# The last layers' first weight pieces asked for on GpSimd, and two of them converted ahead of the first square

## The chip, the core and the metric

The kernel runs on one core of a Trainium2 chip. The metric is the device time of one execution in microseconds (us); the median of three runs is taken. A core has TensorE (PE: matrix products; PEld: its weight loads), VectorE (DVE), ScalarE (ACT), GpSimd (POOL) and SyncE (SP), each working through its own queue of instructions in order, and 16 DMA engines that move data between the large memory and the core's own. SP, ACT and POOL can ask for transfers.

## The reference

Three stages, one after the other: an attention over pooled keys and values, a mixture of experts with one expert a token and a limit on the tokens of an expert, and a dense pair of layers. The change lies in the dense pair:

```
def _moe2_ref(x, w_in, w_out, s, b):        # x: 2304 x 512
    h = x @ w_in                            # w_in: 512 x 2048
    r = np.maximum(h, 0.0)
    g = s * (r * r) + b
    return (g @ w_out).astype(np.float32)   # w_out: 2048 x 512
```

The inputs are 64-bit floats in memory. Tokens over an expert's limit have x = 0; their output row is b times the column sums of w_out.

## The kernel before

**Stages.** Attention, then `Experts.main` (the experts' units of 288 tokens, then small units of up to 144), then `last_layers`. Which units exist depends on the routing, so they stand in nested conditionals; `last` closes the small units. It stores the last small unit's result from the tile `yo` (`store_small`, `store_y`, the SP transfer at L1101), and TensorE computes the first four blocks (`EARLY`) of token unit 0 there.

**Precision.** Every product of the dense pair is three matmuls in a 32-bit format: high half times high half, high times low, low times high. Tokens are split into halves by `split_y` (ScalarE casts, L1014; another engine subtracts, L1015). The pieces of `w_out` are split by `split_out`: ScalarE casts (L1374), VectorE subtracts (L1375).

**Converting w_out.** A piece is 128 rows of `w_out`, 512 KB of 64-bit floats, loaded as pairs of integers by `load_out` (L1446). `Weights64.step` makes 32-bit floats of it in four steps: L859, L862 with ScalarE's L861, L864, L868, of which the second also runs `split_out` for the piece before and the third adds the piece before to the column sums (`add`, L1380; for the first piece a copy on ScalarE, L1382). Two integer buffers c_f and one buffer c_u are shared by all pieces. `cvs` holds two such sequences: 14 pieces (59 steps, `steps_of_first`) and 2 pieces. `conv(n, end)` runs the next n steps, up to `end`.

**last_layers.** The 2,048 columns of the first layer are 16 blocks; the second layer sums over the same 16. Token units are 256 wide. `pair` treats units 0 and 1 together, so that the conversion has more to lie beside: `first(u, f0, f1, banks)` computes blocks of the first layer, each followed by `square` (ScalarE's Relu, L1399, and VectorE's product, L1400, which for every third block writes back into the bank) and by one step `conv(1)`; during unit 0 it also splits unit 1's tokens on VectorE (blocks 10 to 13). `parts` of the block before casts it (L1414) and subtracts (L1415, on GpSimd, or on VectorE for every third). `second` is the second layer (`layer2`, L1420) over two token halves, with `conv(2)` after each block. The order is: 16 blocks of unit 0, 7 of unit 1 (`HEAD`), the second layer over 7 blocks for unit 0 and for unit 1, the last two pieces' loads, unit 1's other 9 blocks, and the rest of the second layer. Unit 0's blocks go around all 8 banks, unit 1's around 4. After `pair`, the units from 2 on go one by one.

**Memory.** `last_layers` takes its tiles from a pool `n`, opened where the experts' pools `m` and `m1` stood before they were closed (L1590 to L1598). `m1` held `yo`; `m` held the experts' weights and raw pieces of `w_in`. `onesf`, y1h, y1l, c_f, c_u, gh, gl and the tiles `wo` are in `n`. The order on each queue is the order in which the program is written; waits are put in by the framework.

**Around the change.** In `pair` SP asks for pieces 0 to 5, then the tokens of unit 1 (`load_y(1)`, L1009 and L1010), the scalars s and b (L1455), and pieces 6 to 13. `nc.gpsimd.memset(onesf, 1.0)` (L1459) is GpSimd's first instruction of the stage.

Of the kernel before, what the change touches and what calls it, by code (L numbers as in the profile page):

```python
# [24 lines left out]
P = 128  # L25
# [10 lines left out]
KF2 = FF2 // P  # L36
# [1313 lines left out]
def last_layers(nc, tc, c, a, pool, x, ps, out):  # L1350
# [6 lines left out]
    sb = pool.tile([P, 2], F32, name="sb")  # L1357
# [6 lines left out]
    wo = [pool.tile([P, DM, 2], I32, name=f"wo{i}") for i in reversed(range(KF2))][::-1]  # L1364
# [5 lines left out]
    wout = a["moe2_w_out"].bitcast(I32).rearrange("(k p) c -> p k c", p=P)  # L1370
# [18 lines left out]
    def conv(n, end=len(steps)):  # L1389
        for _ in range(n):  # L1390
            if done[0] < end:
                z, i = steps[done[0]]
                z.step(i)
                done[0] += 1

    def square(f, p, n, inside=False):

        r = rt[f % 4][:, :n]
        nc.scalar.activation(r, p, AF.Relu)  # L1399
        nc.vector.scalar_tensor_tensor(out=p if inside else r, in0=p, scalar=0.0, in1=r, op0=ALU.max, op1=ALU.mult)  # L1400
# [9 lines left out]
    def parts(f, n=CU, u=0, p=None):  # L1410

        h, l = place(f, u)
        r = rt[f % 4][:, :n] if p is None else p
        nc.scalar.copy(h[:, :n], r)  # L1414
        (nc.gpsimd if p is None else nc.vector).tensor_sub(l[:, :n], r, h[:, :n])  # L1415

    def layer2(p, j, f, c=slice(0, DM), u=0):
        h, l = place(f, u)
        for i, (g, z) in enumerate(((h, 0), (h, 1), (l, 0))):
            nc.tensor.matmul(p[:, c], lhsT=g[:, j * P:j * P + P], rhs=wo[f][:, z, c], start=f == 0 and i == 0, stop=f == KF2 - 1 and i == 2)  # L1420
# [12 lines left out]
    def tokens(u):  # L1433
        if u < NV:
            for k in range(KD):
                x.split_y(u, k, nc.gpsimd)
# [5 lines left out]
        nc.vector.tensor_scalar(out=drop, in0=p, scalar1=sb[:, 1:2], scalar2=None, op0=ALU.mult)  # L1442
        nc.sync.dma_start(out=out.rearrange("(n p) d -> p n d", p=P), in_=drop.unsqueeze(1).to_broadcast([P, T // P, DM]))

    def load_out(i):
        nc.sync.dma_start(out=wo[i].rearrange("p c two -> p (c two)"), in_=wout[:, i])  # L1446

    def pair():

        for i in range(KF2 - 2):  # L1450
            load_out(i)
            if i == 5:
                x.load_y(1)
                for j, n in enumerate(("moe2_s", "moe2_b")):
                    nc.sync.dma_start(out=sb[:, j:j + 1], in_=a[n].unsqueeze(0).to_broadcast([P, 1]))  # L1455
        more.extend(pool.tile([P, 2, 2, CU], F32R, name=f"wo{i}") for i in range(KF2 - 2, KF2))
        spare.extend(x.w.tile([P, 2, CU], F32R, name=f"raw{i}") for i in range(3))
        held = []
        nc.gpsimd.memset(onesf, 1.0)  # L1459

        def first(u, f0, f1, banks):
            for n, f in enumerate(range(f0, f1)):
                p = banks[f % len(banks)][:, :CU]
                if u or f >= EARLY:
                    x.layer1_y(u, p, *win[f])
                inside = f % 3 == 2
                square(f, p, CU, inside)
                conv(1, steps_of_first)
                if u == 0 and 10 <= f < 10 + KD:
                    x.split_y(1, f - 10, nc.vector)  # L1470
                if held:
                    parts(*held.pop())
                held.append((f, CU, u, p if inside else None))
            parts(*held.pop())

        def second(u, f0, f1, end):
            for f in range(f0, f1):
                for j in range(2):
                    layer2(po[2 * u + j], j, f, u=u)
                conv(2, end)  # L1480

        steps_of_first, all_steps = cvs[0].total, len(steps)
        first(0, 0, KF2, ps)
        first(1, 0, HEAD, ph)
        x.load_y(2)
        second(0, 0, HEAD, steps_of_first)
        second(1, 0, HEAD, steps_of_first)
        for i in range(KF2 - 2, KF2):
            wo[i] = pool.tile([P, DM, 2], I32, name=f"wo{i}")
            load_out(i)  # L1490
        first(1, HEAD, KF2, ph)
        conv(all_steps, steps_of_first)
        second(0, HEAD, KF2, all_steps)
        tokens(2)
        second(1, HEAD, KF2, all_steps)
        conv(all_steps)
        raw[0:3] = [x.w.tile([P, DM], F32, name=f"raw{i}") for i in range(3)]
        slots.extend(raw[2:4] + [pool.tile([P, DM], F32, name="c_f1")])
        sums["drop"] = pool.tile([P, DM], F32, name="c_u0")

    def unit(u):
        if u == 2:
            pair()
        if u + 1 < NV:
            x.load_y(u + 1)
        for f in range(KF2):
            p = ph[f % 4][:, :CU]
            x.layer1_y(u, p, *win[f])
            square(f, p, CU)
            if f:  # L1510
                parts(f - 1)
            if u == 2:
                if f == 1:
                    rows(ph[(f + 3) % 4])
                elif f > 11:
                    store((f - 12) // 2, f % 2, po[f - 12])
        parts(KF2 - 1)
        tokens(u + 1)
        if u == 2:
            for f in range(len(slots)):  # L1520
                whole(f)
        for j in range(2):
            p = po[2 * (u % 2) + j]
            for f in range(KF2):
                layer2(p, j, f)
            store(u, j, p)
# [93 lines left out]
```

## Time and profile before

| | us |
|---|---|
| median of three runs | 662.55 (661.93 to 668.51) |
| the profiled execution, its own time | 665.48 |
| its span, first to last instruction | 663.8 |
| TensorE busy | 596.7 |
| VectorE busy | 377.2 |
| ScalarE busy | 254.1 |
| GpSimd busy | 241.9 |

The profile is of one execution. Times in the trace count from the span's start. A busy time of TensorE is modelled, since matmuls are pipelined. A name ahead of "<-" is what is written, names behind it what is read. What ended a wait is inferred from semaphore events: where the engine named had long been done, it was another. `pair` runs from about 340 us, the last small unit's store included, to about 445 us.

### The profile page before, as it was taken

How to read it: one execution, taken by the hardware profiler on the slowest of the kernel's cores; microseconds unless marked ns; L12 is line 12 of the kernel's file. 1: busy time of each engine (PE TensorE's matmuls, PEld its weight loads, DVE VectorE, ACT ScalarE, POOL GpSimd, SP SyncE). 2: the span in 40 equal slices, each digit the busy share in tenths (PEclk: the TensorE clock that was granted, in tenths of full speed). 3: DMA queues.
4: the chain of work that ended last, by engine and by line, in shares of the span. 5: the costliest groups of instructions: out<-in, count | busy, mean ns of one | idle time of the engine just before them, and what ended most of it. 6: DMA issues, size and time to landing. Idle time of an engine off the chain costs nothing. (4 is left out here: it accounts for less than half of the span.)

```text
span 663.8 us, 11041 instructions
## 1 busy us (share of the span) xinstructions
PE 596.7 (90%) x4005; PEld 554.0 (83%) x4005; DVE 377.2 (57%) x889; ACT 254.1 (38%) x620; POOL 241.9 (36%) x277
## 2 busy tenths in 40 slices
PE   5778889689999969997999896999999999999886
PEld 5767778579889969997899776889889899898785
DVE  4699788976979977572719999703412022021150
ACT  1344555435555644434317524404214134043030
POOL 5467232532324503213204401214825336044291
PEclk8798789869999998998999898999999999999998
DMA  8988466645736995756438301017210100100000
GB/s 166 206 166 180 116 171 208 207 149 191 260 131 224 295 284 178 246 172 226 148 91 349 124 1 63 1 32 285 90 39 1 48 17 1 48 17 2 35 1 20
DMA packets 67949, 86.10 MB, mean 130 GB/s; under 512 B 24713, under 2 KB 40073, under 8 KB 67856
## 3 DMA queue, kind: packets, MB, share of 16 engines
q1 hardware_dynamic: 57696, 71.34, 35.5%
q10 hardware_dynamic: 7712, 6.84, 3.5%
q0 software_dynamic: 2448, 6.82, 3.3%
q8 instruction: 42, 0.69, 0.4%
q14 instruction: 51, 0.42, 0.2%
HBM read 68.09 MB, written 17.58 MB: 129 GB/s over the span
## 5 line engine op out<-in xcount | busy, mean ns | idle before, releaser
L1420 PE MATMUL bank<-wo,gh 128*128 128x512 f32 (+1 forms) x412 | 119.2, 374 | 1.2 <-ACT wo L1374 1.0
L1415 POOL TENSOR_TENSOR gl<-rt,gh 128x256 fp32r<-128x256 f32 (+1 forms) x96 | 72.6, 761 | 110.3 <-ACT gh L1414 59.2
L1420 PEld LDWEIGHTS bank<-wo,gh 128*128 128x128 f32 x412 | 74.9, 188 | 15.0 <-ACT wo L1374 1.4
L1420 PE MATMUL bank<-wo,gl 128*128 128x512 f32 (+1 forms) x206 | 76.8, 373 | 0.0
L1096 PE MATMUL bank<-hs,w2h 128*128 128x288 f32 (+1 forms) x308 | 69.1, 313 | 6.1 <-issue 5.7
L1427 DVE SCALAR_TENSOR_TENSOR raw<-bank,sb,c_u 128x512 f32<-128x512 f32 (+1 forms) x14 | 9.9, 710 | 85.5 <-PE bank L1420 85.5
L918 POOL TENSOR_TENSOR w1l<-kraw,w1h 128x512 fp32r<-128x512 f32 x24 | 34.0, 1432 | 64.8 <-ACT w1h L914 64.4
L1096 PEld LDWEIGHTS bank<-hs,w2h 128*128 128x128 f32 x308 | 51.3, 194 | 7.1 <-issue 6.5
L1399 ACT ACTIVATE rt<-tq 128x256 f32<-128x256 f32 (+1 forms) x26 | 9.5, 367 | 113.1 <-PE tq L1022 91.1
L1096 PE MATMUL bank<-hs,w2l 128*128 128x288 f32 (+1 forms) x148 | 45.1, 305 | 0.0
L1420 PEld LDWEIGHTS bank<-wo,gl 128*128 128x128 f32 x206 | 38.8, 188 | 6.8
L1400 DVE SCALAR_TENSOR_TENSOR rt<-bank,rt 128x256 f32<-128x256 f32 (+1 forms) x53 | 21.3, 401 | 38.5 <-ACT rt L1399 38.2
L1414 ACT CAST gh<-rt 128x256 fp32r<-128x256 f32 (+1 forms) x96 | 36.6, 381 | 6.5 <-DVE rt L1400 6.5
L926 POOL DMA_INDIRECT xg<-xd,u_idx x23 | 25.8, 1122 | 35.9 <-DVE lt L283 18.7
L1399 ACT ACTIVATE rt<-bank 128x256 f32<-128x256 f32 (+1 forms) x60 | 22.3, 371 | 35.2 <-PE bank L1022 25.7
L1428 POOL DMA_INDIRECT out_dram<-raw,it x12 | 12.0, 1003 | 62.6 <-DVE raw L1427 62.1
L264 PE MATMUL o<-vx,eT 128*128 128x146 f32 (+1 forms) x144 | 23.5, 309 | 7.8 <-DVE lt L283 7.2
L1400 DVE SCALAR_TENSOR_TENSOR rt<-tq,rt 128x256 f32<-128x256 f32 (+1 forms) x24 | 9.6, 400 | 36.4 <-ACT rt L1399 36.4
L1096 PEld LDWEIGHTS bank<-hs,w2l 128*128 128x128 f32 x148 | 28.7, 194 | 0.0
L264 PEld LDWEIGHTS o<-vx,eT 128*128 128x128 f32 (+1 forms) x144 | 20.2, 194 | 9.1 <-issue 7.1
L922 DVE TENSOR_TENSOR w2l<-vraw,w2h 128x512 fp32r<-128x512 f32 x39 | 26.8, 688 | 1.0 <-ACT w2h L921 0.5
L949 PE MATMUL bank<-xs,w1h 128*128 128x288 f32 (+1 forms) x120 | 26.1, 302 | 1.3 <-DVE hs L952 1.3
(485 smaller groups left out, 1723.7 us busy)
## 6 DMA issues: line engine op xcount, KB each, us to landing
kraw<-in_moe_w_dram SPq DMA_DIRECT2D x14, 1024.0 KB
vraw<-in_moe_w_dram SPq DMA_DIRECT2D x14, 1024.0 KB
wo<-in_moe_w_out_dram SPq DMA_DIRECT2D x16, 512.0 KB
c_raw<-in_moe_w_in_dram ACTq DMA_DIRECT2D x13, 512.0 KB
kraw<-in_k_dram SPq DMA_DIRECT2D x8, 576.0 KB
out_dram<-c_u SPq DMA_DIRECT2D x1, 4608.0 KB
q<-in_q_dram SPq DMA_DIRECT2D x16, 256.0 KB
xd<-xr SPq DMA_DIRECT2D x16, 256.0 KB
```

The source lines that it names most:

```text
L264: nc.tensor.matmul(o[:n, p // 2, p % 2 * 2 * VW:p % 2 * 2 * VW + 2 * VW], lhsT=et[:, p, :n], rhs=two_cols(vx[g][:, 2 * p:2 * p + 2]), star ...
L918: eng.tensor_sub(self.w1l[:, i], self.w1(i), self.w1h[:, i])
L922: eng.tensor_sub(self.w2l[i], self.w2r[:, i], self.w2h[i])
L926: self.nc.gpsimd.indirect_dma_start(out=dst, out_offset=None, in_=self.xd[:have], in_offset=bass.IndirectOffsetOnAxis(ap=idx[:n], axis=0), ...
L949: self.nc.tensor.matmul(p, lhsT=l[:, f, k], rhs=r[k], start=n == 0, stop=n == 3 * KD - 1)
L1096: nc.tensor.matmul(py[d][:, :v.n], lhsT=l[f][:, d * P:d * P + P], rhs=r[f], start=f == 0 and i == 0, stop=f == KF - 1 and i == 2)
L1399: nc.scalar.activation(r, p, AF.Relu)
L1400: nc.vector.scalar_tensor_tensor(out=p if inside else r, in0=p, scalar=0.0, in1=r, op0=ALU.max, op1=ALU.mult)
L1414: nc.scalar.copy(h[:, :n], r)
L1415: (nc.gpsimd if p is None else nc.vector).tensor_sub(l[:, :n], r, h[:, :n])
L1420: nc.tensor.matmul(p[:, c], lhsT=g[:, j * P:j * P + P], rhs=wo[f][:, z, c], start=f == 0 and i == 0, stop=f == KF2 - 1 and i == 2)
L1428: i = nc.gpsimd.indirect_dma_start(out=dst, out_offset=bass.IndirectOffsetOnAxis(ap=ids, axis=0), in_=o[:, c], in_offset=None, bounds_chec ...
```

## The change

`load_out` gets the queue as an argument. In `pair` GpSimd asks for pieces 0 to 5; the token load and the scalars are SP's first requests, and pieces 6 to 13 follow them. Ahead of `first(0, ...)` eight conversion steps are put, so that all later calls of `conv` run eight steps further on.

```diff
-    def load_out(i):
-        nc.sync.dma_start(out=wo[i].rearrange("p c two -> p (c two)"), in_=wout[:, i])
+    def load_out(i, queue=nc.sync):
+        queue.dma_start(out=wo[i].rearrange("p c two -> p (c two)"), in_=wout[:, i])
 
     def pair():
 
-        for i in range(KF2 - 2):
+        for i in range(6):
+            load_out(i, nc.gpsimd)
+        x.load_y(1)
+        for j, n in enumerate(("moe2_s", "moe2_b")):
+            nc.sync.dma_start(out=sb[:, j:j + 1], in_=a[n].unsqueeze(0).to_broadcast([P, 1]))
+        for i in range(6, KF2 - 2):
             load_out(i)
-            if i == 5:
-                x.load_y(1)
-                for j, n in enumerate(("moe2_s", "moe2_b")):
-                    nc.sync.dma_start(out=sb[:, j:j + 1], in_=a[n].unsqueeze(0).to_broadcast([P, 1]))
...
         steps_of_first, all_steps = cvs[0].total, len(steps)
+        conv(8)
         first(0, 0, KF2, ps)
         first(1, 0, HEAD, ph)
```

## Rows read from the trace of the kernel before

**Rows 1.** The page: the chain that ended last, by engine.
```profile
PE 29%; issue 5%; POOL 2%; ACT 1%; DVE 1%; another core or an unknown queue 0%; POOLq 0%; ACTq 0%
```

**Rows 2.** Windows: length, busy PE, PEld, DVE, ACT, POOL, granted clock, DMA share, GB/s.
```profile
365.00:370.00 5.00, 1.98 (x14) 1.58 (x14) 5.00 (x11) 2.46 (x8) 2.36 (x2) 0.99 0.78 311
370.00:375.00 5.00, 5.00 (x31) 5.00 (x31) 4.63 (x11) 3.14 (x8) 2.09 (x3) 0.67 0.40 109
...
410.00:415.00 5.00, 3.70 (x19) 3.41 (x20) 5.00 (x11) 3.38 (x9) 2.30 (x3) 0.59 0.00 0
```

**Rows 3.** Timeline of PE, around the token halves: start, us, engine, instruction, [idle before].
```profile
369.00 0.38 PE L1022 MATMUL tq<-y1l,w1h 128*128 128x256 f32 x1 [2.64 <-DVE y1l L1015]
```

**Rows 4.** Timeline of PE, the first layer's last blocks for unit 1.
```profile
410.05 0.38 PE L1022 MATMUL bank<-y1h,w2h 128*128 128x256 f32 x1 [3.81 <-DVE rt L1400]
...
413.52 0.58 PE L1022 MATMUL tq<-y1h,w2h 128*128 128x256 f32 x1 [1.24 <-DVE gl L1415]
...
421.03 0.63 PE L1420 MATMUL bank<-wo,gh 128*128 128x512 f32 x2
```

**Rows 5.** Who waited for whom from 320 to 350 us: total, times, longest.
```profile
POOL onesf L1459 <- ACT rt L1399: 11.9, 1, 11.9
...
DVE c_f L859 <- DMA wo<-in_moe_w_out_dram: 6.0, 1, 6.0
```

**Rows 6.** Timeline of all engines and of DVE: VectorE's first instructions of the stage.
```profile
342.84 0.43 DVE L1400 SCALAR_TENSOR_TENSOR rt<-tq,rt 128x256 f32<-128x256 f32 x1 [3.56 <-ACT rt L1399]
...
349.25 0.43 DVE L859 TENSOR_SCALAR c_f<-wo 128x512 int32<-128x512 int32 x1 [5.99 <-DMA wo<-in_moe_w_out_dram]
349.60 0.42 DVE L1400 SCALAR_TENSOR_TENSOR rt<-misc,rt 128x256 f32<-128x256 f32 x1
349.93 0.68 DVE L862 SCALAR_TENSOR_TENSOR c_f<-wo,c_f 128x512 int32<-128x512 int32 x1
```

**Rows 7.** Timeline of SP's requests.
```profile
341.25 0.39 SPq L1101 DMA_DIRECT2D yt<-yo  x1
345.01 4.25 SPq L1446 DMA_DIRECT2D wo<-in_moe_w_out_dram  x6
349.31 0.64 SPq L1009 DMA_DIRECT2D yr<-yt  x1
```

**Rows 8.** What SP's queue waited for from 340 to 370 us.
```profile
SPq L1446 <- DMA yt<-yo: 1.8, 1, 1.8
```

**Rows 9.** Timeline of POOL.
```profile
344.78 0.21 POOL L1459 MEMSET onesf<- 128x128 f32 x1 [11.91 <-ACT rt L1399]
```

**Rows 10.** Windows of one microsecond (columns as in the windows above).
```profile
344.00:345.00 1.00, 1.00 (x11) 1.00 (x11) 0.00 (x0) 0.22 (x1) 0.21 (x1) 1.00 0.00 0
...
351.00:352.00 1.00, 1.00 (x11) 1.00 (x10) 1.00 (x2) 0.65 (x3) 1.00 (x2) 1.00 1.04 393
```

**Rows 11.** Lines L926 and L1446: duration ns minimum/median/maximum; landing is L926's.
```profile
L926 POOL DMA_INDIRECT xg<-xd,u_idx x23: 927/980/2152, 111.9 to 311.4; - x23
...
DMA to landing us min/median/max: 4.0/6.7/7.9
...
L1446 SPq DMA_DIRECT2D wo<-in_moe_w_out_dram x16: 327/345/1750, 345.0 to 400.6; - x16
```

**Rows 12.** Timeline of DVE: one piece of the conversion, and the later square.
```profile
398.76 0.42 DVE L859 TENSOR_SCALAR c_f<-wo 128x512 int32<-128x512 int32 x1
...
400.14 0.69 DVE L1375 TENSOR_TENSOR wo<-c_f,wo 128x512 fp32r<-128x512 f32 x1 [0.23 <-ACT wo L1374]
400.75 0.68 DVE L864 SCALAR_TENSOR_TENSOR c_f<-wo,c_f 128x512 int32<-128x512 int32 x1
...
402.56 0.42 DVE L859 TENSOR_SCALAR c_f<-wo 128x512 int32<-128x512 int32 x1
...
409.58 0.42 DVE L1400 SCALAR_TENSOR_TENSOR rt<-bank,rt 128x256 f32<-128x256 f32 x1
```

**Rows 13.** The chain that ended last, in order of time: start, us, what.
```profile
418.48 2.72 PE bank L1022 x24
```

## Prediction

> **What bounds the kernel now.** I read the page first: the chain that ended last is for the greatest part TensorE's, so a change counts only where TensorE stands still or is slowed [rows 1]. The windows of five microseconds around the start of the last layers show where that is: TensorE is busy for 2.0 of the 5 us from 365 and for 3.7 of those from 410, and its granted clock falls (0.67 from 370, 0.59 from 410) [rows 2]. In these windows VectorE is busy for 4.6 to 5.0 of 5 us. So VectorE sets the pace here, and TensorE waits for it twice: 2.64 us for the last low half of unit 1's tokens (L1015, the matmul at 369.00) and 3.81 us for a square (L1400 at 409.58, the matmul at 410.05) [rows 3, 4].
>
> VectorE's busy stretch has a sharp beginning. After its first square at 342.84 it waits 6.0 us for the first piece of w_out, and its first conversion step (L859) starts at 349.25 [rows 5, 6]. This idle stretch is what the change could fill.
>
> Why is the piece late? SP issues the store of the last small unit (L1101) at 341.25 and the first w_out load (L1446) at 345.01, after a wait of 1.8 us that the trace puts down to that store's landing [rows 7, 8]. GpSimd's next instruction is as telling: the memset of `onesf` (L1459), a new tile that needs nobody's data, stands ready from 332.87 and starts at 344.78, after 11.9 us [rows 5, 9]. The view names a Relu (L1399) as its releaser, which a fresh constant does not need; the DMA engines were empty from 344 to 345, so the store's bytes had moved by 344, and the memset starts next [rows 10]. I read it so: `onesf`, `wo` and the buffers c_f and c_u all lie in the pool `n`, opened on the memory that `m` and `m1` gave up, and the first instruction of any engine that touches `n` waits until the last user of that memory is done. That last user is the store out of `yo`, a tile of `m1`.
>
> **The change part by part.**
>
> *The six requests on GpSimd.* In program order they take the memset's place as GpSimd's first instruction on pool `n`. By the reading above they wait where the memset waited, until 344.78, not 332.87: they are not ahead of the store in time, only 0.2 us ahead of SP's request of before. Then each has to be issued. No row shows a plain load from GpSimd; the nearest is its gather L926, median 0.98 us of GpSimd an issue [rows 11], against SP's six issues in 4.25 us, 0.35 the median of one. From the end of an SP issue to the first use took 349.25 - 345.36 = 3.89 us [rows 6, 7]. So the first piece is there at 344.78 + 0.98 + 3.89 = 349.65. In its way comes SP, which no longer has to issue the six pieces first: the token load of unit 1 (512 KB), asked for at 349.31 before, goes out at about 345, and 512 KB at the 393 GB/s of [rows 10] is 1.3 us. If all of that goes ahead of the piece it is there at 350.95. I take the middle, 350.3. Bounds from the gather's own landing times, 4.0 to 7.9 us [rows 11]: 348.8 to 352.7. So VectorE starts 1.05 us later than at 349.25 (from -0.45 to +3.45). The other five requests occupy GpSimd to about 351; it has nothing else to do by then (its first subtraction needs the first square), and the memset's 0.21 us move behind them for nothing.
>
> A rule of the Trainium skill speaks against this part: DMA: Bandwidth & Descriptors, section Issuing engines are not separate DMA queues, says that transfers issued by different engines end on the same 16 DMA engines and interleave, so that a second issuer saves only issue time. The same page's fit for a GpSimd load (2.0 us and the bytes over 436 GB/s) makes 512 KB an estimated 3.2 us, by which the first piece would be there at 348.0 and the total below 2.3 us smaller; no row of before shows such a load.
>
> *The remaining SP loads.* `load_y(1)`, the two scalars and pieces 6 to 13 start some 4 to 6 us earlier. The token load's first use stands behind ten blocks of `first`, the pieces' behind the six before them; neither is waited for where VectorE sets the pace, so nothing is gained.
>
> *conv(8) ahead of the first square.* Two pieces are eight steps. From one L859 to the next (398.76 to 402.56) a piece costs VectorE 3.80 us, in which L1375 takes 0.61 to its successor; L1380, of the same shape, is put at as much [rows 12]. The chain that matters is VectorE's, from its first conversion step to the square at 409.58. It is one queue in order and nearly without gaps (a wait of some 0.23 us in each piece, [rows 12]), so its length is the sum of what stands in it, in whatever order. Before, 51 steps stand in it (16 in the first 16 blocks, 7 in the next 7, 14 and 14 in the two `second` calls). After, all 59 steps of the first 14 pieces do, since they run 8 ahead and their number is bounded. The added eight are L868 of piece 12, the four steps of piece 13 with L1375 and L1380 of its predecessor, and the last L1375 and L1380: 0.60 (at the pace of its neighbours) + 3.80 + 0.61 + 0.61 = 5.6 us. And the first square, which ran in the idle stretch before, now stands in the chain: 0.33 us at the pace of its neighbours [rows 6].
>
> The same eight steps no longer stand behind that square. There TensorE waited 1.24 us for a subtraction (L1415) that was queued among them [rows 4]; I count that back.
>
> Sum at 421.03, where TensorE takes up the second layer again [rows 4]: 1.05 + 5.6 + 0.33 - 1.24 = **+5.7 us**. What lies ahead of that on TensorE is hidden by this chain: it finds no free bank at about 352 (eight blocks computed, the first square not before 355.8), and it stands still for some 4 us there, where it ran on before; the token halves (L1015) come about 8 us later. Both are waits for VectorE in the chain already counted. If VectorE were not the bound, they would be the loss themselves.
>
> The profiled execution took 665.48 us with a span of 663.8; the sum makes it 671.2. The median of the runs shown is 662.55 (661.93 to 668.51), 2.9 below; carried over, the prediction is 662.55 + 5.7 = **668.2 us**.
>
> **The rivals.**
>
> *First: the requests are not held by the store* (not slower). What speaks for it is the code: the first pieces are the last tiles of `n` and lie in what was `m`, on weights and raw pieces that nothing reads after 332. Against it stands the memset. Even then VectorE cannot start at 338, because c_f, which its first step writes, is in the pool too and waits as the memset did: it starts at 345.0, 4.25 us earlier instead of 1.05 later: -4.25 + 5.6 + 0.33 - 1.24 = +0.4, 663.0 us. It decides from a first step at 344.6 on downwards; only then is there a gain, and the store's landing excludes that.
>
> *Second: the piece comes later still.* GpSimd's issue takes longer than a gather's, or the piece shares the way with the token load and with SP's pieces 6 onwards for its whole length. At the gather's longest landing, 7.9 us, the step is at 352.7: 3.45 + 5.6 + 0.33 - 1.24 = +8.1, 670.7 us. The gather's median of 6.7 us speaks for it (351.5, +6.9); but gathers ran beside other large loads.
>
> *Third: the clock.* The five blocks from 410.05 to 421.03 are 60 matmuls. Less the wait of 1.24 they took 9.7 us; at the pace of the last 24 of them, 2.72 us [rows 13], they would take 6.8. The other 2.9 us are the clock, which fell to the lower level of 1.2 GHz for a part of them (0.59 granted from 410 to 415) after the stand of 3.81 us [rows 2, 4]. I expect a stand before the same square again, and so the same loss: TensorE gets the last token half 8 us later, at 377, and took 37 us from there to the stand; so it stops at about 414, and the square comes at 416.6. It is a shorter stand, 2.6 us. If the clock holds, 5.7 - 2.9 = +2.8, 665.4 us.
>
> **How the numbers follow.** Forecast (held by the store, first step from 348.8 to 351.2) 0.60; second rival 0.22; third 0.10; first 0.08. About 1% (6.6 us) is what a measurement of this kernel can tell from no change. The forecast reaches from +4.2 to +6.6 in most of its cases, a fifth beyond; with most of the second rival that makes 0.35 for slower by more. Faster by over 1% would need a first step at about 338, and has 0.04 for what I overlook; 0.61 is left for within 1%. The range goes from just below the first rival, 662.5, to past the second's price, 672.5.
>
> **What would show it.** GpSimd's first w_out request starts at 344.8, not near 333; VectorE's first L859 at 349 to 352 with eight steps ahead of its first L1400, at about 355.8; TensorE stands still at 352 and longer before the token halves; the square of block 7 of unit 1 near 416.6, and no conversion step behind it until L1420 resumes near 426.7. I am wrong if the request starts before 342, if L859 starts before 346, or if VectorE's queue shows gaps of several microseconds between its first step and that square, for then it is not a sum.

## The result, and the profile after

The changed kernel takes 672.58 us (median; 670.07 to 675.94) beside 662.24 us (661.36 to 668.51) for the kernel before in the same runs. The ratio is **1.0135** (95% interval 1.0102 to 1.0168), so the change costs 8.9 us (6.8 to 11.1): 1.0135 times the 662.55 us shown before is 671.5 us. The quotient of the two medians alone is 1.0156, inside that interval. The forecast was 668.2. The profiled execution has a span of 670.9 us, against 663.8.

GpSimd, timeline (start, us, engine, line, instruction, count, [idle before <- releaser]):

```profile
344.60 3.26 POOL L1446 DMA_DIRECT2D wo<-in_moe_w_out_dram  x6 [12.52 <-issue]
347.85 0.22 POOL L1460 MEMSET onesf<- 128x128 f32 x1
```

SP, timeline (same columns):

```profile
340.52 0.39 SPq L1101 DMA_DIRECT2D yt<-yo  x1
343.79 0.37 SPq L1009 DMA_DIRECT2D yr<-yt  x1
...
346.89 4.21 SPq L1446 DMA_DIRECT2D wo<-in_moe_w_out_dram  x6
```

The store of the last small unit (L1101) is asked for 0.73 us earlier in this execution than in the one of before [rows 7], so instants are compared below as distances from that store. GpSimd's first request is 4.08 us behind it; SP's was 3.76 behind it [rows 7]. GpSimd stood idle for 12.5 us ahead of it and gained nothing: the request waits where the memset waited [rows 9]. The six requests take 3.26 us, 0.53 us the median of one. SP asks for the tokens 0.8 us ahead of GpSimd's first request, and for the later pieces 2.3 us behind it.

VectorE, timeline (same columns):

```profile
350.83 0.43 DVE L859 TENSOR_SCALAR c_f<-wo 128x512 int32<-128x512 int32 x1 [11.41 <-DMA wo<-in_moe_w_out_dram]
...
356.70 0.42 DVE L1400 SCALAR_TENSOR_TENSOR rt<-tq,rt 128x256 f32<-128x256 f32 x1
...
412.45 0.69 DVE L868 SCALAR_TENSOR_TENSOR c_f<-c_u,c_f 128x512 f32<-128x512 f32 x1
...
417.69 0.69 DVE L1375 TENSOR_TENSOR wo<-c_f,wo 128x512 fp32r<-128x512 f32 x1 [0.74 <-ACT wo L1374]
418.30 0.68 DVE L1380 TENSOR_TENSOR raw<-raw,c_f 128x512 f32<-128x512 f32 x1
418.90 0.42 DVE L1400 SCALAR_TENSOR_TENSOR rt<-bank,rt 128x256 f32<-128x256 f32 x1
...
430.06 0.42 DVE L859 TENSOR_SCALAR c_f<-wo 128x512 int32<-128x512 int32 x1
```

The first conversion step comes 10.31 us behind the store (8.00 before, [rows 6, 7]), the first square stands behind eight steps, and the square of block 7 of unit 1 comes at 418.90 instead of 409.58 [rows 12]. From 412.45 to 418.90 there are 6.45 us of conversion that no longer stand behind that square; no step follows it until 430.06.

TensorE, timeline (same columns):

```profile
357.17 0.80 PE L1022 MATMUL tq<-yhl,w2h 128*128 128x256 f32 x2 [5.69 <-DVE rt L1400]
...
378.87 0.58 PE L1022 MATMUL tq<-y1l,w1h 128*128 128x256 f32 x1 [2.63 <-DVE y1l L1015]
...
419.37 0.58 PE L1022 MATMUL bank<-y1h,w2h 128*128 128x256 f32 x1 [4.38 <-DVE rt L1400]
```

Windows (length, busy PE, PEld, DVE, ACT, POOL, granted clock, DMA share, GB/s):

```profile
355.00:360.00 5.00, 2.83 (x13) 2.83 (x14) 4.96 (x10) 3.77 (x11) 1.57 (x2) 0.64 1.03 419
360.00:365.00 5.00, 5.00 (x30) 4.78 (x30) 5.00 (x10) 2.94 (x9) 2.38 (x3) 0.68 1.03 411
...
420.00:425.00 5.00, 5.00 (x26) 5.00 (x26) 1.52 (x4) 1.74 (x7) 2.08 (x3) 0.53 0.00 0
```

TensorE now stands three times for VectorE: a new 5.69 us before the first square's bank is free, the token halves, and block 7's square, for 4.38 us instead of 3.81 [rows 3, 4]. After each longer stand the granted clock is low (0.64 and 0.68, then 0.53).

Where the time went, with every link read as a difference of instants in the trace (a first step is the first L859, square 7 the square of block 7 of unit 1, and L1420 the instant at which the second layer is taken up again). For the last two kernels, which have no store there, the start is the end of ScalarE's four copies into `yo`, 0.03 us ahead of the store in the others. In the two kernels that move the store it is the first half's request.

| kernel | start | start to first w_out request | request to first step | first step to square 7 | square 7 to L1420 | sum, less before | time by the ratio |
|---|---|---|---|---|---|---|---|
| before | 341.25 | 3.76 | 4.24 | 60.33 | 11.45 | | |
| after | 340.52 | 4.08 | 6.23 | 68.07 | 9.87 | +8.5 | +8.9 |
| e1, GpSimd's requests alone | 342.31 | 4.38 | 5.07 | 61.26 | 11.60 | +2.5 | +2.7 |
| e2, eight steps alone | 340.18 | 3.91 | 4.64 | 68.21 | 9.93 | +6.9 | +5.3 |
| e3, steps capped | 339.68 | 3.97 | 4.50 | 61.79 | 9.69 | +0.2 | -0.5 |
| e4, all loads on GpSimd | 337.56 | 4.18 | 4.40 | 67.72 | 11.33 | +7.9 | +11.5 |
| e5, store elsewhere | 341.69 | 2.74 | 3.99 | 59.28 | 9.69 | -4.1 | -3.6 |
| e8, adds on GpSimd | 337.20 | 3.89 | 4.58 | 62.03 | 9.45 | +0.2 | -0.9 |
| e9, e5 and e8 | 338.60 | 2.71 | 3.77 | 61.41 | 9.44 | -2.4 | -4.4 |
| e12, before without the late store | 341.67 | 0.07 | 3.88 | 60.18 | 11.20 | -4.5 | -2.1 |
| e13, after without the late store | 342.90 | 0.64 | 6.30 | 68.46 | 10.14 | +5.8 | +7.2 |

The last column is the ratio less 1, times 662 us; its interval is 1.7 to 3.6 us to either side. The sums lie within it or at most 0.2 us outside, but for e4's (0.5 us outside; its profiled execution, 669.25 us, was faster than its median of 674.44). So these four links hold what the change does. Each is read from one execution, though, and two cautions go with the table. The changed kernel and e1 make the same requests in the same order, and yet their links from request to first step differ by 1.16 us. And the last link depends on TensorE's granted clock in it, which was 0.69 to 0.72 in most kernels, 0.82 in e5, e8 and e9 and 1.00 in e3.

### The profile page after: what moved, and what is told of

Same layout as the page of the kernel before. It is cut to its first block, busy times and chain, and to the rows that moved or that the text cites. A ratio compares the mean times of both kernels' runs of the same rounds, so it can differ in the third digit from the quotient of the medians.

```text
span 670.9 us, 11044 instructions
## 1 busy us (share of the span) xinstructions
PE 595.1 (89%) x4005; PEld 552.3 (82%) x4005; DVE 377.9 (56%) x889; ACT 253.5 (38%) x620; POOL 244.1 (36%) x283
## 5 line engine op out<-in xcount | busy, mean ns | idle before, releaser
L1420 PE MATMUL bank<-wo,gh 128*128 128x512 f32 (+1 forms) x412 | 118.9, 373 | 0.0
L1420 PEld LDWEIGHTS bank<-wo,gh 128*128 128x128 f32 x412 | 74.9, 188 | 13.1
L1420 PE MATMUL bank<-wo,gl 128*128 128x512 f32 (+1 forms) x206 | 76.8, 373 | 0.0
L1420 PEld LDWEIGHTS bank<-wo,gl 128*128 128x128 f32 x206 | 38.8, 188 | 6.9
L926 POOL DMA_INDIRECT xg<-xd,u_idx x23 | 25.9, 1127 | 32.8 <-DVE r L279 15.6
L219 PE MATMUL sc<-kbd,qT 128*128 128x144 f32 (+1 forms) x152 | 24.6, 309 | 5.8 <-DVE rmine L369 4.3
L219 PEld LDWEIGHTS sc<-kbd,qT 128*128 128x128 f32 (+1 forms) x152 | 21.5, 197 | 7.4 <-issue 6.6
```

The lines of the kernel that those rows point to most:

```text
L219: nc.tensor.matmul(sc[:n, p // 2, p % 2 * 144:p % 2 * 144 + 144], lhsT=q[:, p, :n], rhs=kbd[b % 2][:, p], start=True, stop=True)
L926: self.nc.gpsimd.indirect_dma_start(out=dst, out_offset=None, in_=self.xd[:have], in_offset=bass.IndirectOffsetOnAxis(ap=idx[:n], axis=0), ...
```

## The experiments

**One part at a time: e1_gpsimd_only and e2_steps_only.** The first is the changed kernel without the steps ahead, the second the kernel before with nothing but them.

```diff
 # e1: the changed kernel
-        conv(8)
```

```diff
 # e2: the kernel before
         steps_of_first, all_steps = cvs[0].total, len(steps)
+        conv(8)
```

> The requests alone: GpSimd asks for the first six pieces, no steps ahead of the first square. Theory (VectorE's queue is a sum, and the requests only move its beginning): in the changed kernel the first L859 stands 10.31 us behind the last small unit's store (340.52 to 350.83), before it was 8.00 (341.25 to 349.25). The same 10.3 here, so 2.3 us more than before: about 664.6 us, ratio 1.0035. Rival (the requests on GpSimd are the larger part of the loss of some 9 us): ratio 1.008 or more.

> The eight steps alone, all loads on SP in the order of before. Theory: the first L859 stands 8.0 us behind the store as before; the square of block 7 of unit 1 (at 409.58 before) comes 5.9 to 7.7 us later, because eight steps more and one square stand ahead of it in VectorE's queue; 1.2 to 1.6 us are given back behind it. 4.7 to 6.2 us in all, ratio 1.007 to 1.009. Rival (the steps are harmless or useful, only the late pieces cost): within 1 us of before, ratio 0.998 to 1.002.

e1: 1.0041 (1.0011 to 1.0070). e2: 1.0080 (1.0052 to 1.0107). Both parts cost by themselves, 2.7 and 5.3 us, and 8.0 together, near the 8.9 of the whole change. That one hides or helps the other can't be told within their intervals (1.9 and 1.8 us to either side). In e1 the first step comes 9.45 us behind the store, not after the expected 10.3. e2 also shows what the memset waits for, which the view of before named wrongly [rows 5]. GpSimd and SP in e2:

```profile
343.86 0.21 POOL L1459 MEMSET onesf<- 128x128 f32 x1 [13.88 <-DMA yt<-yo]
```

```profile
340.18 0.39 SPq L1101 DMA_DIRECT2D yt<-yo  x1
344.09 4.34 SPq L1446 DMA_DIRECT2D wo<-in_moe_w_out_dram  x6
```

**The order without the added steps: e3_steps_capped.** Eight steps run ahead, but the two calls of `second` stop eight short, so that as many steps as before stand ahead of square 7.

```diff
+        conv(8)
 ...
-        second(0, 0, HEAD, steps_of_first)
-        second(1, 0, HEAD, steps_of_first)
+        second(0, 0, HEAD, steps_of_first - 8)
+        second(1, 0, HEAD, steps_of_first - 8)
```

> The eight steps ahead as in the run with the steps alone, but the two calls of second stop eight steps earlier, so that 51 steps stand ahead of the square of block 7 as before, and the last eight lie one behind each later block as before. Theory (sum): the loss of the eight steps is gone but for the moved square, 0.3 us, and what the order itself costs: 0.3 to 2 us above before, ratio 1.0005 to 1.003, though TensorE still stands still for some 4 us at 352 and longer ahead of the token halves. Rival (that early stand of TensorE, and the later token halves, are the loss): as with the steps alone, ratio 1.007 to 1.009.

0.9993 (0.9968 to 1.0018). TensorE and windows in e3:

```profile
354.48 0.80 PE L1022 MATMUL tq<-yhl,w2h 128*128 128x256 f32 x2 [4.24 <-DVE rt L1400]
...
376.19 0.58 PE L1022 MATMUL tq<-y1l,w1h 128*128 128x256 f32 x1 [2.64 <-DVE y1l L1015]
```

```profile
375.00:380.00 5.00, 3.81 (x18) 3.81 (x19) 4.60 (x10) 1.43 (x5) 1.59 (x2) 0.50 0.39 108
...
410.00:415.00 5.00, 4.96 (x43) 4.76 (x42) 5.00 (x12) 3.54 (x10) 1.74 (x3) 1.00 0.00 0
```

The early stand of TensorE is here too (4.24 us, and a clock of 0.50 later), yet the time is that of before. So that stand is not the loss by itself. VectorE's chain grew by only 61.79 - 60.33 = 1.46 us; the eight steps ahead of square 7 make up the rest, 68.07 - 61.79 = 6.3 us between e3 and the changed kernel. In the changed kernel the early stand is hidden under that chain: TensorE stands for another 4.38 us before square 7, and would only stand longer if it came there sooner. In e3 nothing is left to hide it. The stand before square 7 is gone, and TensorE, which has no wait left behind the token halves (the last that the trace lists ends at 376.19), sets the pace to L1420 itself. The windows from square 7 to L1420, before, in the changed kernel and in e3:

```profile
409.58:421.03 11.45, 9.73 (x60) 9.44 (x61) 9.11 (x20) 5.90 (x16) 4.07 (x5) 0.70 0.00 0
```

```profile
418.90:428.77 9.87, 9.40 (x61) 9.40 (x61) 3.89 (x11) 4.27 (x13) 3.23 (x5) 0.71 0.00 0
```

```profile
409.94:419.63 9.69, 9.65 (x82) 9.45 (x81) 9.14 (x20) 6.12 (x17) 4.03 (x5) 1.00 0.00 0
```

At a full clock TensorE ran 82 matmuls in 9.65 us, 22 of them left over from ahead of square 7; before, it ran 60 of the same line and shape in 9.73 us at 0.70. At e3's pace 60 would take 7.1 us, so the clock is worth some 2.7 us here (an estimate from these two rows). In e3 loss and gain cancel on TensorE: it takes up the last token half 36.51 us behind the store instead of 27.75 [rows 3], and L1420 43.44 us behind that instead of 52.03.

**What makes the first piece late: e4_all_on_gpsimd.** e1 with the token load, the scalars and pieces 6 to 13 asked for by GpSimd too, so that piece 0 has nothing beside it when it starts.

```diff
-        x.load_y(1)
+        x.load_y(1, nc.gpsimd)
 ...
-            nc.sync.dma_start(out=sb[:, j:j + 1], in_=a[n].unsqueeze(0).to_broadcast([P, 1]))
+            nc.gpsimd.dma_start(out=sb[:, j:j + 1], in_=a[n].unsqueeze(0).to_broadcast([P, 1]))
 ...
-            load_out(i)
+            load_out(i, nc.gpsimd)
```

> No steps ahead of the first square; GpSimd asks for everything (pieces 0 to 5, the token load, the scalars, pieces 6 to 13), so that nothing of SP's goes beside the first piece. From GpSimd's first request to VectorE's first L859 it took 6.2 us in the changed kernel and 5.1 with the requests alone, and 4.2 to 4.6 where SP asks. Theory (the first piece shares the way with SP's token load and pieces): 4.2 to 4.8 us here, ratio 1.000 to 1.002. Rival (a request of GpSimd takes longer by itself): 5.1 us or more, ratio 1.003 or more.

From GpSimd's first request to the first step 4.40 us, as the theory of sharing had it. The windows of exactly that stretch show the sharing in bytes. First the changed kernel, then e4, then the kernel before (columns as above):

```profile
344.60:350.83 6.23, 6.23 (x55) 6.23 (x54) 0.00 (x0) 0.07 (x1) 3.47 (x7) 1.00 0.92 276
```

```profile
341.74:346.14 4.40, 4.40 (x41) 4.40 (x40) 0.00 (x1) 0.07 (x1) 4.39 (x8) 1.00 0.66 231
```

```profile
345.01:349.25 4.24, 4.24 (x39) 4.24 (x38) 0.00 (x0) 0.06 (x1) 0.00 (x0) 1.00 0.63 191
```

Length times rate is 1.72 MB in the changed kernel, 1.02 in e4 and 0.81 before; one piece is half a megabyte (512 KB). The DMA engines are no slower; they are busier, with other loads. Which loads, the view of DMA queues tells for the changed kernel's 6.23 us (queue, kind: packets, MB, share of 16 engines; q0 is GpSimd's, q1 SP's):

```profile
q0 software_dynamic: 314, 1.17, 56.1%
q1 hardware_dynamic: 903, 0.53, 34.5%
```

SP's 0.53 MB at the 276 GB/s of this stretch are 1.9 us, about what e4's first step is sooner (6.23 - 4.40 = 1.83). But bytes are not all of it: in e1 SP's queue moved 0.52 MB up to the first step as well, at the same 276 GB/s, and the step came after 5.07 us. What was moved first tells more. The queues in the 3.00 us behind GpSimd's first request, in the changed kernel, in e1 and in e4 (columns as above):

```profile
q1 hardware_dynamic: 750, 0.52, 68.4%
q0 software_dynamic: 19, 0.08, 18.8%
```

```profile
q1 hardware_dynamic: 528, 0.52, 59.3%
q0 software_dynamic: 68, 0.28, 24.3%
```

```profile
q0 software_dynamic: 109, 0.43, 47.4%
```

SP's 0.52 MB are the token load, 512 packets of 1 KB: it goes ahead of the piece nearly whole. SP's later pieces are not in the way, since up to the first step SP's queue moved no more than the token load and small packets, in the changed kernel, e1 and e13 alike. The changed kernel and e1 differ by SP's other packets in these 3 us, 238 against 16, which are those of the small loads asked for behind the tokens (L1010 and the scalars); e13, with 6.30 us, has 221, and 0.08 MB on GpSimd's queue. That these small packets hold up the piece is not isolated by any run.

But e4 as a whole is slower, 1.0174 (1.0126 to 1.0222), where its expectation had no change, and the cause is another queue. GpSimd in e4:

```profile
348.92 0.53 POOL L1447 DMA_DIRECT2D wo<-in_moe_w_out_dram  x1 [1.07 <-DMA wo<-in_moe_w_out_dram]
...
355.07 2.09 POOL L1447 DMA_DIRECT2D wo<-in_moe_w_out_dram  x4 [0.82 <-DMA yr<-yt]
357.15 0.22 POOL L1461 MEMSET onesf<- 128x128 f32 x1
357.32 2.54 POOL L1416 TENSOR_TENSOR gl<-rt,gh 128x256 fp32r<-128x256 f32 x3
```

ScalarE, then VectorE:

```profile
358.09 0.38 ACT L1400 ACTIVATE rt<-bank 128x256 f32<-128x256 f32 x1 [9.68 <-POOL gl L1416]
```

```profile
358.51 0.43 DVE L1401 SCALAR_TENSOR_TENSOR rt<-bank,rt 128x256 f32<-128x256 f32 x1 [8.65 <-ACT rt L1400]
```

GpSimd's later requests wait for earlier loads to land, and its subtractions queue behind them until 357.3. ScalarE's next Relu waits 9.68 us for the first of them, and VectorE 8.65 us for that Relu. SP, which computes nothing, had no such work behind its requests.

**A store out of another tile: e5_store_elsewhere.** The kernel before, with the last small unit's result copied into the raw tiles of pool `w` and stored in two halves, each behind its own two copies.

```diff
-            store_small(s)
+            store_last(s)
 ...
+        def store_last(s):
+            for i in range(2):
+                y = self.raw[1 + i][:, 0:2 * SM].rearrange("p (k c) -> p k c", k=2)
+                for d in range(2):
+                    nc.scalar.copy(y[:, d], py[2 * i + d][:, :SM])
+                nc.sync.dma_start(out=self.yt.rearrange("(d p) n -> p d n", p=P)[:, 2 * i:2 * i + 2, cols(sid(s), SM)], in_=y)
```

> The kernel before, but the last small unit's result is stored out of two tiles of another pool (raw1, raw2, in two transfers), so that the store is no longer the last user of the memory that pool n takes over. Theory (the first requests wait for the store to land because of that memory): SP's first w_out request follows the stores at once, near 342.1 instead of 345.0, GpSimd's memset starts near 341 instead of 344.78, VectorE's first L859 comes at about 346.4, and the time falls by about 2.9 us: ratio 0.9955. Rival (something else holds the requests, such as the end of the conditionals): memset and request where they were, ratio 1.000.

0.9946 (0.9915 to 0.9978): faster than both kernels, and nearly as expected, but not for the reason expected. GpSimd in e5:

```profile
344.61 0.21 POOL L1466 MEMSET onesf<- 128x128 f32 x1 [12.66 <-DMA yt<-raw]
```

The memset still waits for the store, though the store no longer reads a tile of `m1`; so the reading that the memory of `m1` ties the two is refuted. The store, in halves of which the first is asked for behind two copies instead of four, lands sooner: 2.74 us from the first half's request to SP's first w_out request, against 3.76. That is only 1.0 of the 4.1 us in the table. Another 1.05 lie in a shorter chain, whose cause was not traced, and 1.76 in the stretch to L1420, which TensorE ran at a granted clock of 0.82, not 0.70.

**The adds on GpSimd: e8_adds_on_gpsimd and e9_adds_and_store.** If VectorE's queue is the bound, taking the sums L1380 off it during the two calls of `second` should shorten it.

```diff
-            nc.vector.tensor_add(raw[3], raw[3], f)
+            adds[0].tensor_add(raw[3], raw[3], f)
 ...
+        adds[0] = nc.gpsimd
         second(0, 0, HEAD, steps_of_first)
         second(1, 0, HEAD, steps_of_first)
+        adds[0] = nc.vector
```

> The kernel before, but the column sums (L1380) of the seven pieces converted beside the first two calls of second are added on GpSimd, which does nothing there. Theory (VectorE's queue from its first step to the square of block 7 is a sum): seven times 0.60 us leave it, 4.2 us, less what its other steps lose beside GpSimd (a subtraction took 1.22 instead of 0.69 us in such a place), some 2 us: ratio 0.994 to 0.9975. Rival (the square of block 7 is held by something else, or the slowed steps eat it all): ratio 0.999 to 1.002.

> The same with the store of the last small unit from the other pool, in two halves (ratio 0.9946 by itself). Theory: the two add up, one moves the beginning of VectorE's queue and one shortens it: 0.9946 and the gain of the adds, ratio 0.989 to 0.992. Rival (they gain the same microseconds): no better than 0.9946.

e8: 0.9987 (0.9957 to 1.0017), no gain. In e8's timeline of all engines:

```profile
384.86 1.33 POOL L1382 TENSOR_TENSOR raw<-raw,c_f 128x512 f32<-128x512 f32 x1 [2.63 <-DVE c_f L868]
385.08 1.65 DVE L862 SCALAR_TENSOR_TENSOR c_f<-wo,c_f 128x512 int32<-128x512 int32 x1
```

Before, L862 stands alone (VectorE, timeline):

```profile
384.04 0.69 DVE L862 SCALAR_TENSOR_TENSOR c_f<-wo,c_f 128x512 int32<-128x512 int32 x1
```

L862 takes 1.65 us beside GpSimd's sum, where alone it takes 0.69. Six of them take 1.65 to 1.68 us ahead of square 7, 5.8 us more in all, while the seven sums had taken 4.2: the chain is 62.03 us long, 1.7 longer than before. L862 ends at 386.73, 0.54 us after GpSimd's sum (386.19): it looks held rather than slowed. That is what the Trainium skill states in SBUF — State Buffer, section Who interferes with whom: a VectorE instruction with two inputs in the on-chip memory and a GpSimd instruction that reads it exclude each other, and the later one waits. e9: 0.9934 (0.9908 to 0.9961), overlapping e5's interval, where 0.989 to 0.992 was expected: no gain of both over e5 alone can be told.

**No store under way: e12_no_late_store and e13_change_no_late_store.** e5 had left open what the requests wait for. Here nothing is stored at the end of the last small unit; the other buffer goes out earlier instead, so those columns of the result hold another unit's numbers. Both kernels get the same edit.

```diff
 # in last(s)
             early = cap >= SM + CU
+            nc.sync.dma_start(out=self.yt.rearrange("(d p) n -> p d n", p=P)[:, :, cols(sid(s), SM)], in_=yo((s + 1) % 2, SM))
             small_numbers(s)
 ...
-            store_small(s)
+            store_y(sid(s), yo(s % 2, SM), SM, False)
```

> The kernel before, but the store of the last small unit (L1101, 341.25 in the kernel before) is not issued at the end of that unit. In its place the same number of bytes, the other buffer's contents, goes out to the same columns some 15 us earlier, ahead of small_numbers; those columns of the result therefore hold another unit's numbers. ScalarE's four copies out of PSUM stay where they are. So no store is under way when pool n opens. Theory (it is the landing of that store, and nothing else, for which the first GpSimd and SP instructions of the last layers wait): onesf's memset and SP's first w_out request start as soon as ScalarE's copies are done, at about 341.3 to 342.0 instead of 344.78 and 345.01 with the stage starting alike; by the 4.24 us from request to the first conversion step of before (345.01 to 349.25) that step comes at 345.5 to 346.3, 3 to 3.7 us sooner, and if all of that reaches the end the ratio is 0.9945 to 0.9960. Rival 1 (they wait for something else that ends there too): the requests stay at 344.5 to 345.0 and the ratio is 0.999 to 1.001. Rival 2 (the requests come sooner, but VectorE's chain then stands before TensorE instead, as where the steps were capped): the first step sooner by 3 us or more, but the ratio 0.998 or more.

> The changed kernel with the same edit (the last small unit's store replaced by one of the other buffer some 15 us earlier; those columns of the result hold another unit's numbers). Theory (the landing holds GpSimd's first request too): that request starts at about 341.0 to 342.0 instead of 344.60, and the first conversion step comes 4.4 us later (measured from request to step where nothing shared the way) up to 6.2 us later (where SP's loads shared it): 345.5 to 348.2 instead of 350.83. The eight steps cost what they cost, so the ratio to the kernel before falls from 1.0135 by 2.6 to 5.0 us, to 1.006 to 1.0095. Rival 1: the request stays at 344.6 and the ratio at 1.012 to 1.015. If the early request is all that the change needs to work, the first step here comes sooner than in the kernel before with the same edit; if asking on GpSimd and letting SP's token loads go beside it costs more than it saves, it comes later.

GpSimd in e12, then in e13:

```profile
341.77 0.21 POOL L1461 MEMSET onesf<- 128x128 f32 x1 [9.81 <-ACT yo L1100]
```

```profile
343.54 3.26 POOL L1448 DMA_DIRECT2D wo<-in_moe_w_out_dram  x6 [10.53 <-ACT yo L1100]
```

Without the store both start within 0.1 and 0.64 us of ScalarE's last copy, instead of 3.8 to 4.1 behind it: the store's landing is the wait. All of it reaches the first step of e12 (3.95 us from the start, 8.00 before) and L1420 (-4.5 us). In the time that is not as clear: e12's ratio is 0.9969 (0.9933 to 1.0004), with the expected 0.9945 to 0.9960 inside the interval and no change at its edge; the profiled span, 658.7 us, is 5.1 shorter. The edit has a small price of its own: the token load for unit 0 now waits for the early store, and TensorE for that load, 0.38 us. e13 is at 1.0108 (1.0053 to 1.0163), above its expected 1.006 to 1.0095, which its interval takes in.

The pair answers the question in e13's last expected sentence. With nothing in the way of the request, the way over GpSimd still brings the first step 6.94 us behind the start, where SP's brings it after 3.95. By these two executions the change's first part would be a loss of 3.0 us even if its premise held.

## Why the prediction fell short: right mechanism, two terms too small

*VectorE sets the pace* held. In every kernel of the table but e4 the chain from the first step to square 7 has no gap over 0.74 us, and in the changed kernel its length moves the end: TensorE stands 4.38 us before square 7 in spite of its new early stand. The forecast had this stand shorter than before, 2.6 us, in part since it had the chain too short. In e3 alone, with the early stand but without the added steps, TensorE has no stand there and sets the pace.

*The requests are not ahead of the store* held, and the first rival fell: 344.60, where 344.8 was forecast; e12 and e13 show that it is the landing. The reason given, memory that `m1` gave up, is refuted by e5. What ties the first instructions on pool `n` to the store when the store reads another pool is not settled by these runs.

*The first piece* was forecast 1.05 us later and came 2.31 later (10.31 against 8.00 behind the store), inside its bounds. What was off in it is the sharing. The forecast had put between nothing and the whole token load, 1.3 us, ahead of the piece, and took the middle, 0.65. In fact the whole load goes ahead, and the piece is 1.83 us later than in e4, where nothing of SP's is beside it (6.23 against 4.40). The issue was put too high, 0.98 us for 0.53. The two errors point opposite ways, and the sharing is the larger. Its size is not steady: e13 has 6.30 us, but e1, with the same requests, 5.07, only 0.67 above e4. The prediction had no term for the small loads between the tokens and the later pieces, which is where these executions differ (e4 above); whether they are the cause stays open. The second rival named this mechanism; its price (a first step at 352.7) was too high, the step came at 350.83.

The Trainium skill says, in DMA: Bandwidth & Descriptors, section SWDGE vs HWDGE vs iDMA, that GpSimd's and SP's transfers feed different queues of each DMA engine, which serves them in turn. The traces list two queues, q0 and q1; turns they do not show, and in the first 3.00 us the bytes were far from even, 0.08 MB on GpSimd's queue and 0.52 on SP's.

*Eight steps more ahead of square 7, and the first square in the chain*, were put at 5.93 us and the chain grew by 7.74. Busy time and gaps over the chain, before and after (windows):

```profile
349.25:409.58 60.33, 52.19 (x338) 47.33 (x336) 57.95 (x108) 30.82 (x76) 15.40 (x16) 0.97 0.39 145
```

```profile
350.83:418.90 68.07, 53.37 (x318) 48.45 (x316) 64.35 (x117) 33.09 (x81) 15.92 (x16) 0.89 0.31 115
```

VectorE is busy 6.40 us longer and idle 1.34 us longer (3.72 less 2.38). The steps themselves took 6.45 us (412.45 to 418.90), not 5.6: the last L1375 waits 0.74 us for ScalarE's cast (L1374), since no step of a next piece lies between them. The remaining 7.74 - 6.45 = 1.3 us are the reordering: e3, which has the order without the added steps, has 1.46. Of that 0.33 was forecast for the first square. Two gaps of 0.46 and 0.32 us before squares at 382.74 and 384.82, in which VectorE waits for a Relu of a late block, are in the changed kernel where before had one of 0.37; the last half microsecond or so was not traced further. So "a sum in whatever order" was right to about 1 us in 60, and that is what was missing.

*Given back*: 1.24 forecast, 11.45 - 9.87 = 1.58 measured. The third rival (a clock that holds) fell: the clock is 0.53 from 420 to 425, and 0.71 from square 7 to L1420 against 0.70 before. Its price was about right: the rival had 2.9 us, and e3's full clock is worth some 2.7 (windows above).

Together: 2.31 + 7.74 - 1.58 = 8.5 us against 5.7. All three signs were right, as were the places; 671.5 lies inside the range, which ends at 672.5; the median of 672.58 lies just past that end. "Slower by over 1%", which had 0.35, is what came out, not "within 1%" with 0.61: the spread given to the forecast, 4.2 to 6.6 us, came from the first piece alone. The chain's term of 5.93 had been given no bounds, and it was the one that missed most.

## What to carry to other kernels

Before a request is moved to an idle queue, look for another instruction of that queue which waits without need of data: here a memset showed that GpSimd would wait as SP did. When a single in-order engine is the bound, price a reordering by what newly stands ahead of the instruction that others wait for, and add the wait at the new seam, where nothing is left to lie between a producer and its user. And when a second queue asks for loads of its own at the same time, those can go first: SP had moved 0.52 MB of tokens when GpSimd's queue had moved 0.08 MB of the pieces that VectorE stood waiting for.

## What the runs showed of the hardware that was not expected

- A plain 512 KB load costs GpSimd 0.53 us an issue, little more than half of its gather's 0.98 [rows 11], but later requests wait on GpSimd for earlier loads (0.26 to 1.72 us each in e4) and hold up its arithmetic.
- From the request to the first use, 512 KB took 3.77 to 4.64 us over SP (e9, e2) and 4.40 over GpSimd alone, and 5.07 to 6.30 over GpSimd with SP's token load beside it (e1, e13).
- VectorE's L862, 0.69 us by itself, took 1.65 to 1.68, six times, while GpSimd ran a sum of the same size (e8).
